# Attention into SwiGLU on one core: seven half-size products for 16 more chunks, with every side step placed by a written list

## The chip, the cores and the metric

One core of a Trainium2 chip runs the whole program. The metric is the device time of one execution, in microseconds (us); the kernel before took 926.79 us as the median of three runs (926.09 to 927.77).

## The reference, cut to what matters

```python
# q, k, v: (B=8, H=8, S=576, D=64); keys and values are averaged over windows of 8 -> 72 per head
k_p = k.reshape(B, H, 72, 8, D).mean(axis=3);  v_p = v.reshape(B, H, 72, 8, D).mean(axis=3)
scores = np.matmul(q, k_p.transpose(0, 1, 3, 2)) / np.sqrt(D)
attn = np.exp(scores - scores.max(-1, keepdims=True));  attn = attn / (attn.sum(-1, keepdims=True) + 1e-9)
x = np.matmul(attn, v_p).transpose(0, 2, 1, 3).reshape(4608, 512)      # B*S tokens, H*D channels
g = x @ w_gate                                                        # (512, 1536)
out = (g * sigmoid(g) * (x @ w_val)) @ w_out                          # (1536, 512)
```

All is float32, and the result has to be close to float32. The kernel gets there with pairs of 16-bit numbers (high part and remainder): a product of two such pairs is three matmuls, high times high, high times remainder, remainder times high.

## The kernel before, in words

**Tiles and chunks.** The 4,608 tokens are 9 tiles of 512. The 1,536 hidden channels are 12 chunks of 128. For each tile, chunk after chunk, TensorE makes the gate and the value of 128 hidden channels (both from the 512 input channels), ScalarE, VectorE and GpSimd make the hidden product from them, and TensorE multiplies that by w_out into four PSUM accumulators (`project`, L963: 4 matmuls of the float32 weights with `hh`, then 8 of 16-bit weights with `hb` and `hl`).

**Two ways to make gate and value of a chunk.** The plain way (`side`, L927 to L929) is 12 matmuls with 512 columns for the gate and 12 for the value. The other way (`product`, L1109) treats input channels, gate and value, and the two halves of the tile's tokens as a 2 by 2 block product and makes it from seven products of half the size instead of eight: 7 x 6 = 42 matmuls with 256 columns. It needs sums and differences: of the weights of a chunk (`fast_weights`, once per chunk) and of the tile's input (`fast_x`, once per tile, in two halves). Per chunk it also needs three copies on ScalarE (`keep_fast` L1424, `seed_fast` L1429, L1488) and two additions on VectorE (`second_fast` L1435, L1492), and its remainder `hl` (L1400) is made on GpSimd instead of VectorE. `READY` gives the number of chunks that go this way in each tile: 5, 7, 9, 9, 9, 9, 12 in tiles 2 to 8. A tile's plain chunks come first. Tile 8 has no plain chunk; its first products begin inside the last chunk of tile 7 (`CROSS`, `begin_fast`).

**The side work.** While TensorE works on tile i, the attention of later tiles' tokens is made, in pieces of at most 128 queries: split the queries (`split_q` L611 to L614), scores on TensorE (L631, L632), less the maximum (L641, L642), exponentials (L653), split them into a `half` buffer (`blocks_high` on ScalarE, the remainders `blocks_low` on GpSimd, L727 and L730), transpose that by a DMA (`turned` L734, `pt<-half` or `pt<-area`), multiply by the values on TensorE (`values_of_heads` L755, L756), divide (L760), split again (L882, L885) and transpose into `x` by a DMA (L890). Each batch also needs its keys and values loaded and summed (`batch_load`, `batch_sum`, `prep`).

**What sets the order.** The order is fixed when the program is built, one queue per engine (PE TensorE, ACT ScalarE, DVE VectorE, POOL GpSimd, SP the DMA queue). The first tile goes by a written list (`ORDER`). From tile 1 on the builder calls `slot` (L1170) between groups of matmuls. It keeps running counts of when each engine will be free (`now`, `spend`), and puts in what fits the room that it is told (`ROOM`, `FAST_ROOM`): sums first, then attention steps and batch steps. Two pieces at most are under way, and the `half` buffers alternate until tile 7 (`SOLO`); from there one of them serves as room for a second tile's input sums.

Of the kernel before, what the change touches and what calls it, by code (L numbers as in the profile page):

```python
# [16 lines left out]
P = 128  # L17
# [34 lines left out]
H8 m9 P8 t14 y12 La2 O12 u14 v14 w13 m10 Pa5 T8 w14 y13 O13 Y8 X8 Z8 y14 Z6 Pa2 A A  # L52
"""
AFTER = {"V": 91312.0, "A": 89862.0, "P": 94264.0}
# [3 lines left out]
EVEN_ON_VECTOR = ('N0', 'N4', 'N8')  # L58
TILE = 512
# [11 lines left out]
CAME = 6000  # L71
URGE = (0, 0)
FAST_ROOM = (3500, 1350), (2550, 2210), (1250, 1050), (950, 180), (3350, 800), (1760, 4190), (2900, 5200)
FAST_FIRST, FAST_THEN = 3, 5
ONE_BANK = (1, 8)
LANDS = 6250
SETTLE = 0
TURNS = 4500
AHEAD = 9
COST = (1.0, 1.0, 0.92)  # L80
# [20 lines left out]
def attention_then_swiglu(  # L101
# [226 lines left out]
    prepped, scaled = set(), set()  # L328
    busy = {"ps": False, "values": False, "sums": False}
# [158 lines left out]
    freed = [0, 0, 0]  # L488

    def batch_load(b, i):  # L490
        src, n, _, _ = batch(b, i)
        state["in", b, i] = mid.tile([P, 2, n], F32, name="in", tag="mid")
        nc.sync.dma_start(out=state["in", b, i], in_=src)
        state["from", b, i] = now["pe"]
        now["loads"] += 1

    def batch_sum(b, i, part=None):
        box(0)
        if i >= 4:
            box(1)  # L500
        for n in (0, 1) if part is None else (part,):
            if i >= 4:
                batch(b, i)[3](state["in", b, i], n)
            elif n == 0:
                batch(b, i)[3](state["in", b, i])
        if part != 0:
            state["in", b, i] = None
            now["loads"] -= 1
            if i < 4:
                spend("P", 2600)  # L510
            freed.append(now["P" if i < 4 else "V"] + SETTLE)

    def prep(b):

        order = 0, 4, 1, 5, 2, 6, 3, 7
        todo = [i for i in order if ("in", b, i) not in state]

        def load():
            if todo and now["loads"] < 2 and not now["hold"] and now["pe"] >= freed[-3]:
                batch_load(b, todo.pop(0))  # L520

        for i in order:
            while (
                i in todo
                or state["in", b, i] and now["pe"] < state["from", b, i] + LANDS
                or i < 4 and any(e["t"][0] == "x" for e in lines["extra"])
            ):
                load()
                yield 0, 0
            for n in (0, 1) if i >= 4 else (None,):  # L530
                if state["in", b, i]:
                    yield (batch(b, i)[2], 0, "same") if n else (batch(b, i)[2], 0)
                    batch_sum(b, i, n)
                    load()
        yield from settle("P")
        mx, ks, vs = state["sizes", b]["t"], home["ks"], home["vs"]
        yield 1300, 0
# [3 lines left out]
        yield 0, 0  # L541
        yield from settle("V")
        while busy["ps"] or (now["one"] and busy["values"]):
            yield 0, 0
        busy["sums"] = True
        sums = over_rows(mx[:, :3])
        yield 400, 0
        pow2_above(p2s[:, b, :3], inv[:, b], sums)
        yield from settle("V")
        busy["sums"] = False  # L550
# [4 lines left out]
        scaled.add(b)  # L555
        while b - 2 in under_way:
            yield 0, 0
        for g in range(2):
            yield (1100, 0, "same") if g else (1100, 0)
            split_k(b, g)  # L560
        for g in range(2):
            for part in range(4):
                yield 650, 0, "same"
                split_v(b, g, part)
        prepped.add(b)

    queries = {}
    now = {"one": False, "job": None, "pe": 0, "V": 0, "A": 0, "P": 0, "loads": 0, "hold": False}

    def spend(engine, n, *after):  # L570
        now[engine] = max(now[e] for e in (engine, "pe", *after)) + n * COST["VAP".index(engine)]

    def settle(*engines, more=SETTLE):
        end = max(now[e] for e in engines) + more
        while now["pe"] < end:
            yield 0, 0
# [198 lines left out]
    def ask(t):  # L775

        i, off, b, s0, m = t["at"]
        t["me"] = turn[0]
        turn[0] += 1
        t["qs"] = box(t["me"])["qs"] if b >= SPLIT else None  # L780
        for g in range(2 if b >= SPLIT else 0):
            for part in range(2):
                yield (0, 700, "same") if g + part else (0, 700)
                split_q(b, s0, m, t["qs"], g, part)
            spend("P", 1080, "A")
        if b >= SPLIT:
            load_next()
            yield from settle("P")

    def front(t):  # L790

        i, off, b, s0, m = t["at"]
        yield 0, 0
        while busy["values"] or busy["sums"]:
            yield 0, 0
        busy["ps"] = True
        sc = None
        for groups in ((0,), (1,)) if now["one"] else ((0, 1),):
            pss = scores(b, s0, m, t["qs"], groups=groups)
            if groups[-1]:  # L800
                if b < SPLIT:
                    load_next()
                t["asked"] = False
            for g in groups:
                yield 900, 0
                sc = less_max(b, m, pss, sc, (g,))
            yield from settle("V")
        busy["ps"] = False
        t["sc"] = sc

    last = {"turned": 0}

    def soft(t):

        i, off, b, s0, m = t["at"]
        half, sc = halves[t["me"] % 2 if now["tile"] < SOLO else 0], t["sc"]
        while now["tile"] >= SOLO and now["pe"] < last["turned"]:
            yield 0, 0
        yield 0, 900
        if b < SPLIT:  # L820
            exponentials(m, sc)
            yield from settle("A")
            yield 1300, 0
            ri = inverse_sums(m, sc)
            yield 750, 0, "same"
            normalise(nc.vector, m, sc, ri)
            yield from settle("V")
            yield 0, 1500
            soft_high(m, sc, half)
            soft_low(m, sc, half)  # L830
            spend("P", 1700, "A")
        else:
            weights(b, m, sc)
            for part in range(4):
                yield 0, (650, 450, 450, 650)[part], "same"
                blocks_high(m, sc, half, part)
            blocks_low(m, sc, half)
            spend("P", 1700, "A")
        yield 0, 0
        t["pt"] = turned(m, half, OLD // P if b < SPLIT else 2 * H)  # L840
        t["turned"] = last["turned"] = max(now["pe"], now["P"]) + TURNS
        if b >= SPLIT:
            yield 750, 0
            sm = row_sums(m, sc)
            yield 600, 0, "same"
            t["ri"] = one_over(m, sm)

    def back(t):

        i, off, b, s0, m = t["at"]  # L850
        yield 0, 0
        while now["pe"] < t["turned"]:
            yield 0, 0
        bs = sorted({sub[1] for sub in tiles[i][2]})
        while not scaled.issuperset(bs) or b not in prepped or any(busy.values()) or now["tile"] < i - 1:
            yield 0, 0
# [3 lines left out]
        if i not in rate:  # L860
            rate[i] = scales(bs, x["mt"])
        r = rate[i][b]
        busy["values"] = True
        if b < SPLIT:
            ps = values(b, m, t["pt"])
            yield 0, 700
            x_high(ps, m, x, off, r)
            yield from settle("A")
            yield 750, 0
            x_low(ps, m, x, off, r)  # L870
            yield from settle("V")
            busy["values"] = False
        else:
            ps = values_of_heads(b, m, t["pt"])
            yield 700, 0
# [728 lines left out]
```

## Time and profile before

| | |
|---|---|
| median of three runs | 926.79 us (926.09 to 927.77) |
| profiled execution, device time | 926.48 us |
| its span | 924.1 us |
| busy: TensorE matmul / weight load | 886.9 / 586.4 us |
| busy: VectorE / ScalarE / GpSimd | 638.0 / 513.8 / 462.7 us |
| granted TensorE clock, mean | 0.996 |

The span runs from the first to the last instruction; the device time is 2.4 us longer. The profile's line numbers are those of the kernel before. The order rows of the change have its own numbers: L1042 is `product`, L916 `project`, L1005, L1009 and L1020 `fast_x`, L741 the transposition of `half`, L853 that into `x`.

### The profile page before, as it was taken

The page shows a single profiled execution, that of the slowest core. Times are in us where ns is not written, and L with a number is a line of the kernel's source. Part 1 is how long each engine was busy: PE and PEld are TensorE (multiplying, and loading weights), DVE is VectorE, ACT ScalarE, POOL GpSimd, SP SyncE. Part 2 cuts the span into 40 slices and gives each one's busy share as a digit, 9 for nine tenths or more (in the row PEclk, how much of TensorE's full clock was granted, in tenths as well). Part 3 has the DMA queues.
Part 4 walks back from the last instruction along what each step waited for, and adds up shares of the span by engine and source line. Part 5 has one row for each costly group of instructions (what it writes and reads, how often), then busy time and mean ns, then how long its engine had stood idle before and what let it go on. Part 6 is the DMA issues. An engine that isn't in the chain of part 4 may idle for free.

```text
span 924.1 us, 16885 instructions
## 1 busy us (share of the span) xinstructions
PE 886.9 (96%) x6414; PEld 586.4 (63%) x6505; DVE 638.0 (69%) x1155; ACT 513.8 (56%) x1081; POOL 462.7 (50%) x520
## 2 busy tenths in 40 slices
PE   4789999999999999999999999999999999999997
PEld 4676445454555575577667765776577757777775
DVE  6899985877767679676867777677755585634233
ACT  2677833375456555746475655665657555444343
POOL 5457966498666944776376332543214416114111
PEclk9899999999999999999999999999999999999999
DMA  9967742257443822863286236732322322101001
GB/s 348 261 221 229 251 117 71 73 170 158 80 140 52 221 57 56 205 154 78 47 192 162 64 71 171 164 91 40 96 54 63 76 69 41 29 1 46 1 1 46
DMA packets 155537, 103.19 MB, mean 112 GB/s; under 512 B 113216, under 2 KB 141888, under 8 KB 153920
## 3 DMA queue, kind: packets, MB, share of 16 engines
q1 hardware_dynamic: 153728, 83.24, 37.4%
q10 hardware_dynamic: 1728, 18.88, 5.5%
q8 instruction: 51, 0.84, 0.4%
q14 instruction: 30, 0.25, 0.1%
HBM read 67.63 MB, written 9.44 MB: 83 GB/s over the span
## 4 chain that ended last, share of the span: by engine, by line
PE 76%; DVE 15%; issue 3%; ACT 2%; DMA 2%; POOL 2%; SPq 0%; ACTq 0%; DVEq 0%; POOLq 0%
PE gv L1109 29%; PE acc L963 24%; PE gv L927 6%; PE gv L929 6%; PE gv L928 6%; DVE mixed L244 2%; DVE wgv_l L278 1%; DVE hf L945 1%; DMA qt<-q_rows 1%; PE ps L631 1%; DVE ws L233 1%; DVE hf L951 1%; PE ps L755 1%; PE ps L632 1%; DVE fx L1057 1%
## 5 line engine op out<-in xcount | busy, mean ns | idle before, releaser
L1400 POOL TENSOR_TENSOR hl<-hf,hh 128x512 bf16<-128x512 f32 x71 | 92.9, 1309 | 198.3 <-ACT hh L1391 198.3
L941 ACT ACTIVATE hf<-gv,un 128x512 f32<-128x512 f32 (+1 forms) x111 | 75.0, 675 | 171.7 <-PE gv L1109 111.8
L963 PE MATMUL acc<-hl,wo_h 128*128 128x512 bf16 (+1 forms) x435 | 161.4, 373 | 2.2 <-issue 0.3
L945 DVE SCALAR_TENSOR_TENSOR hf<-hf,gv 128x512 f32<-128x512 f32 (+1 forms) x111 | 74.4, 670 | 119.3 <-ACT hf L941 119.2
L927 PE MATMUL gv<-x,wgv_h 128*128 128x512 f16 (+1 forms) x408 | 149.6, 367 | 4.5 <-DVE hf L945 3.8
L929 PE MATMUL gv<-x,wgv_l 128*128 128x512 f16 (+1 forms) x408 | 149.5, 366 | 0.5 <-DVE wgv_l L278 0.5
L928 PE MATMUL gv<-x,wgv_h 128*128 128x512 f16 (+1 forms) x408 | 149.5, 366 | 0.5 <-DVE x L770 0.5
L963 PE MATMUL acc<-hh,wo_h 128*128 128x512 f32 (+1 forms) x444 | 130.1, 415 | 0.0
L614 POOL TENSOR_TENSOR box<-qt,box 64x512 f16<-64x512 f32 (+1 forms) x60 | 66.5, 1109 | 105.6 <-ACT box L613 91.8
L963 PE MATMUL acc<-hb,wo_l 128*128 128x512 bf16 x307 | 117.2, 382 | 0.4
L1109 PEld LDWEIGHTS <-mixed 128*128 128x128 f16 x1044 | 101.1, 98 | 25.5 <-issue 0.9
L1109 PEld LDWEIGHTS <-wgv_h 128*128 128x128 f16 x960 | 92.9, 98 | 34.2 <-issue 2.4
L1391 ACT CAST hh<-hf 128x512 fp32r<-128x512 f32 x72 | 44.4, 617 | 117.8 <-DVE hf L951 117.7
L1109 PE MATMUL gv<-area,mixed 128*128 128x256 f16 x696 | 94.9, 273 | 0.0
L1109 PE MATMUL gv<-x,wgv_h 128*128 128x256 f16 x528 | 93.0, 273 | 0.0
L951 DVE SCALAR_TENSOR_TENSOR hf<-gv,un,hf 128x512 f32<-128x512 f32 (+1 forms) x87 | 63.3, 728 | 39.6 <-PE gv L1109 34.0
L963 PEld LDWEIGHTS acc<-hh,wo_h 128*128 128x128 f32 x444 | 76.3, 189 | 14.0 <-ACT hh L1391 0.3
L963 PEld LDWEIGHTS <-wo_l 128*128 128x128 bf16 x444 | 43.2, 97 | 52.1 <-issue 26.3
L1109 PE MATMUL gv<-x,wgv_l 128*128 128x256 f16 x264 | 71.9, 273 | 0.0
L929 PEld LDWEIGHTS <-wgv_l 128*128 128x128 f16 x408 | 39.9, 98 | 44.7 <-DVE wgv_l L278 1.0
L928 PEld LDWEIGHTS <-wgv_h 128*128 128x128 f16 x408 | 39.9, 98 | 42.8 <-issue 5.2
L927 PEld LDWEIGHTS <-wgv_h 128*128 128x128 f16 x408 | 39.9, 98 | 38.1
(203 smaller groups left out, 1883.7 us busy)
## 6 DMA issues: line engine op xcount, KB each, us to landing
ws<-w_all ACTq DMA_DIRECT2D x12, 1536.0 KB, 7.2
qt<-q_twice SPq DMA_DIRECT2D x48, 256.0 KB, 3.1
out_t<-ob SPq DMA_DIRECT2D x36, 256.0 KB, 2.5
in<-k_rows SPq DMA_DIRECT2D x12, 576.0 KB, 5.1
in<-q_rows SPq DMA_DIRECT2D x12, 576.0 KB, 5.1
in<-v_main SPq DMA_DIRECT2D x12, 512.0 KB, 5.0
in<-v_rest SPq DMA_DIRECT2D x12, 512.0 KB, 5.0
qt<-q_rows SPq DMA_DIRECT2D x8, 256.0 KB, 6.2
```

The source lines that it names most:

```text
L244: nc.vector.scalar_tensor_tensor(out=wf.bitcast(U32), in0=wf.bitcast(U32), scalar=3, in1=chunks[c]["low"], op0=ALU.logical_shift_left, op1 ...
L614: nc.gpsimd.tensor_sub(o[rows], qt[rows], o[rows])
L927: nc.tensor.matmul(o, wh, x["h"][:, j, a:e], start=(j == 0), stop=False)
L928: nc.tensor.matmul(o, wh, x["l"][:, j, a:e], start=False, stop=False)
L929: nc.tensor.matmul(o, wl, x["h"][:, j, a:e], start=False, stop=(j == NJ - 1))
L941: nc.scalar.activation(hf, gate, AF.Tanh, scale=un[:, c, 0:1])
L945: nc.vector.scalar_tensor_tensor(out=hf, in0=hf, scalar=1.0, in1=gate, op0=ALU.add, op1=ALU.mult)
L951: nc.vector.scalar_tensor_tensor(out=out, in0=val, scalar=un[:, c, 2:3], in1=hf, op0=ALU.mult, op1=ALU.mult)
L963: nc.tensor.matmul(acc[j][:, a:e], w[:, c, j * P : (j + 1) * P], h[:, :n], start=begin and at < NJ, stop=end and w is wo_up,)
L1109: nc.tensor.matmul(o, a, b, start=begin and j + n == 0, stop=j == HJ - 1 and n == 2, skip_group_check=True,)
L1391: nc.scalar.copy(hh[:, :n], hf)
L1400: eng.tensor_sub(hl[:, :n], hf, hh[:, :n].bitcast(F32))
```

## The change

`READY` becomes 7, 10, 11, 12, 12, 12, 12 for tiles 2 to 8: 16 more chunks by seven half-size products, 76 instead of 60. Tiles 5, 6 and 7 have no plain chunk any more, so their first products, like those of tile 8, begin inside the last chunk of the tile before. One `half` buffer is given up from tile 4 on instead of tile 8 (`SOLO` 3). The running counts go. `slot` now takes its steps from a written list, one group of steps per place, with finer steps: p for a piece of attention, b and l for a batch and its loads, w and x for the sums of weights and of a tile's input, q for the loads of queries.

```diff
-ROOM = (3410, 3290)
-READY = (0,0,5,7,9,9,9,9,12)
-MADE = (0,5,7,9,9,9,9,11)
-LATE = {8:(11,)}
-CROSS = (8,)
-SOLO = 7
+READY = (0, 0, 7, 10, 11, 12, 12, 12, 12)
+CROSS = (5,6,7,8)
+SOLO = 3
+PLAN = """
+p0:2 w0 / w0:3 / w0 b2 p0 / / w0 / / w0 / p0 b2:3 / / / q w0 p0 b2 / / p0 b2:2 p1 w0 / p1 b2 w0
...
-    def slot(vector, scalar):
-        room = {"V": now["pe"] + vector, "A": now["pe"] + scalar}
...
+    steps_of = iter(PLAN.split("/"))
+    def slot():
+        for word in next(steps_of).split():
+            name, _, times = word.partition(":")
+            for _ in range(int(times or 1)):
+                if name not in lines:
+                    lines[name] = line(name)
+                next(lines[name], None)
...
-        while now["tile"] >= SOLO and now["pe"] < last["turned"]:
-            yield 0, 0
...
-        while now["pe"] < t["turned"]:
-            yield 0, 0
...
-            while now["pe"] < came[i][n]:
-                yield 0, 0
```

The step functions issue the same instructions as before (`ask`, `front`, `soft` and `back` are joined into `attend`); only where they stand differs, and a `yield` now ends a step without asking for room. At the end of `ORDER` the two steps `A`, which began the next batch, are gone.

On TensorE, at the start of tile 7, a plain chunk's gate stands before, right behind tile 6's last `project`:

```order
L963 MATMUL acc_7889<-hl,wo_h 128x512
L927 LDWEIGHTS wgv_h
L927 MATMUL gv_8915<-x,wgv_h 128x512
L928 LDWEIGHTS wgv_h
L928 MATMUL gv_8915<-x,wgv_h 128x512
L929 LDWEIGHTS wgv_l
L929 MATMUL gv_8915<-x,wgv_l 128x512
```

and now tile 7's first product of half the size, one chunk earlier in the queue:

```order
L1042 MATMUL gv_9226<-x,wgv_h 128x256
L1042 LDWEIGHTS wgv_h
L1042 MATMUL gv_9226<-x,wgv_h 128x256
L1042 LDWEIGHTS wgv_l
L1042 MATMUL gv_9226<-x,wgv_l 128x256
```

The matmuls have 256 columns where they had 512, and each still has its own weight load.

On VectorE, around the start of tile 7 (`un` marks it). Before, tile 7's input sums (`fx<-x`, `fx<-fx`) follow it:

```order
L951 SCALAR_TENSOR_TENSOR hf<-gv_8782,un,hf 128x512
L1446 TENSOR_TENSOR un<-p2w,mt 128x36
L1057 TENSOR_TENSOR fx<-x 128x2x256 x2
L1064 TENSOR_TENSOR fx<-fx 128x2x128 x4
L908 TENSOR_SCALAR mt<-p2s 128x1
```

Now the second half of these sums stands in the next to last chunk of tile 6, cut in pieces between the chunk's own four operations (L900, L1339, L905, L1293):

```order
L1293 TENSOR_TENSOR gv_9075<-gv_9030,rs 128x256
L666 TENSOR_REDUCE sm<-sc 128x8
L1005 TENSOR_TENSOR fx<-x 128x2x256 x2
L1009 TENSOR_TENSOR fx<-fx 128x2x128 x2
L900 SCALAR_TENSOR_TENSOR hf<-hf,gv_9075 128x512
L1339 TENSOR_TENSOR gv_9030<-gv_9030,rs 128x256
L1009 TENSOR_TENSOR fx<-fx 128x2x128 x2
L905 SCALAR_TENSOR_TENSOR hf<-gv_9030,un,hf 128x512
L1293 TENSOR_TENSOR gv_9173<-gv_9131,rs 128x256
L1020 TENSOR_TENSOR x<-fx,x 128x2x128
L1020 TENSOR_TENSOR area<-fx,area 128x6x128
```

On the DMA queue, the end of tile 6 and the start of tile 7 (`out_t<-ob` writes a finished tile). Before, the transpositions of `half` alternate between two buffers, and the last one into tile 7's `x` stands well behind it:

```order
L584 DMA qt<-q_twice 128x4x128 x2
L734 DMA_TRANSPOSE pt<-area 128x16x64
L584 DMA qt<-q_twice 128x4x128 x2
L734 DMA_TRANSPOSE pt<-half 128x16x128
L890 DMA_TRANSPOSE x<-box 128x8x64
L584 DMA qt<-q_twice 128x4x128 x2
L734 DMA_TRANSPOSE pt<-area 128x16x128
L1121 DMA out_t<-ob 128x512 x4
```

Now all go through one buffer, and the last one into `x` (of 64 queries) has the next piece's transposition right ahead of it:

```order
L741 DMA_TRANSPOSE pt<-half 128x16x64
L853 DMA_TRANSPOSE x<-box 128x8x64
L591 DMA qt<-q_twice 128x4x128 x2
L741 DMA_TRANSPOSE pt<-half 128x16x128
L853 DMA_TRANSPOSE x<-box 128x8x64
L741 DMA_TRANSPOSE pt<-half 128x16x128
L591 DMA qt<-q_twice 128x4x128 x2
L1053 DMA out_t<-ob 128x512 x4
```

The input of tile 7 is now finished and summed before tile 6 ends.

## Rows read from the trace of the kernel before

**Rows 1.** The page: the span and the busy time of each engine.

```profile
span 924.1 us, 16885 instructions
PE 886.9 (96%) x6414; PEld 586.4 (63%) x6505; DVE 638.0 (69%) x1155; ACT 513.8 (56%) x1081; POOL 462.7 (50%) x520
```

**Rows 2.** Busy time of each engine by stretches that are about the tiles (1 to 8 from the second row on); columns: stretch, its length, busy us (instructions) of PE, PEld, DVE, ACT and POOL, granted TensorE clock, DMA share, GB/s.

```profile
0.00:138.00 138.00, 113.64 (x829) 77.27 (x833) 121.35 (x213) 84.03 (x164) 88.23 (x102) 0.98 0.76 239
138.00:258.00 120.00, 118.19 (x704) 61.01 (x711) 87.97 (x147) 58.56 (x116) 83.30 (x93) 1.00 0.45 109
258.00:358.00 100.00, 98.77 (x684) 59.89 (x695) 70.96 (x127) 57.93 (x124) 62.10 (x74) 1.00 0.47 112
358.00:453.00 95.00, 94.08 (x679) 61.48 (x690) 70.47 (x129) 58.50 (x127) 61.12 (x70) 1.00 0.53 124
453.00:548.00 95.00, 94.04 (x742) 65.41 (x753) 68.64 (x129) 58.65 (x129) 52.02 (x58) 1.00 0.52 119
548.00:641.00 93.00, 92.40 (x715) 64.71 (x724) 68.96 (x134) 54.04 (x117) 37.18 (x41) 1.00 0.48 115
641.00:736.50 95.50, 94.60 (x745) 65.75 (x754) 59.38 (x117) 57.48 (x129) 29.84 (x34) 1.00 0.32 70
736.50:831.60 95.10, 94.19 (x705) 66.06 (x715) 59.12 (x111) 48.77 (x103) 29.04 (x32) 1.00 0.15 34
831.60:924.00 92.40, 87.01 (x626) 64.85 (x635) 31.18 (x55) 35.84 (x76) 19.90 (x19) 1.00 0.07 24
```

**Rows 3.** The timeline of TensorE: the first and the last of the twelve matmuls of one plain gate (start, duration, line).

```profile
560.00 0.38 PE L927 MATMUL gv<-x,wgv_h 128*128 128x512 f16 x1
...
562.38 0.38 PE L929 MATMUL gv<-x,wgv_l 128*128 128x512 f16 x1
```

**Rows 4.** The chain of waits in tile 8, in order of time: start, length, what, and how many in a row.

```profile
839.09 2.62 PE gv L1109 x24
...
846.34 2.62 PE gv L1109 x24
```

**Rows 5.** Groups of instructions by form: the weight loads of the half-size products (busy us, mean ns of one, idle before).

```profile
L1109 PEld LDWEIGHTS <-mixed 128*128 128x128 f16 x1044 | 101.1, 98 | 25.5 <-issue 0.9
```

**Rows 6.** The same view: what a chunk costs beside TensorE. Three copies, two additions, the remainder on either engine, and VectorE's two other operations.

```profile
L1424 ACT COPY rs<-gv 128x256 f32<-128x256 f32 x60 | 22.8, 380 | 0.0
L1429 ACT COPY gv<-gv 128x256 f32<-128x256 f32 x60 | 22.3, 372 | 5.0 <-DVE hf L945 3.9
L1488 ACT COPY gv<-gv 128x256 f32<-128x256 f32 x60 | 21.7, 361 | 0.7 <-PE gv L1109 0.4
L1435 DVE TENSOR_TENSOR gv<-gv,rs 128x256 f32<-128x256 f32 x60 | 25.8, 430 | 47.6 <-PE gv L1109 42.6 <-ACT hb L1394 2.8 <-PE ps L213 1.5
L1492 DVE TENSOR_TENSOR gv<-gv,rs 128x256 f32<-128x256 f32 x60 | 25.6, 426 | 2.0 <-ACT gv L1488 2.0
L1400 DVE TENSOR_TENSOR hl<-gv,hh 128x512 bf16<-128x512 f32 x24 | 16.5, 688 | 15.1 <-ACT hb L1394 15.1
L1400 POOL TENSOR_TENSOR hl<-hf,hh 128x512 bf16<-128x512 f32 x71 | 92.9, 1309 | 198.3 <-ACT hh L1391 198.3
L945 DVE SCALAR_TENSOR_TENSOR hf<-hf,gv 128x512 f32<-128x512 f32 x105 | 71.9, 685 | 119.3 <-ACT hf L941 119.2
L951 DVE SCALAR_TENSOR_TENSOR hf<-gv,un,hf 128x512 f32<-128x512 f32 x81 | 60.5, 746 | 39.6 <-PE gv L1109 34.0 <-PE gv L929 3.9 <-POOL wo_l L287 1.0
```

**Rows 7.** The same view: the sums of a tile's input on VectorE with the copy on ScalarE.

```profile
L1057 DVE TENSOR_TENSOR fx<-x 128x512 f32<-128x512 f16 x28 | 20.6, 777 | 0.0
L1064 DVE TENSOR_TENSOR fx<-fx 128x256 f32<-128x256 f32 x32 | 16.8, 525 | 0.8
L1077 ACT CAST x<-fx 128x256 f16<-128x256 f32 x2 | 0.8, 405 | 0.0
L1083 DVE TENSOR_TENSOR x<-fx,x 128x256 f16<-128x256 f32 x2 | 1.8, 891 | 0.6 <-ACT x L1077 0.6
```

**Rows 8.** The page: the DMA transpositions, how many and the median us from issue to landing.

```profile
x<-box SPq DMA_TRANSPOSE x30, 3.6
pt<-half SPq DMA_TRANSPOSE x21, 4.3
```

**Rows 9.** The timeline of GpSimd, the DMA queue and the weight loads at one place of tile 4: the remainders of a piece, its transposition, and the first weight load that reads it, with TensorE's idle time before it in brackets.

```profile
473.25 1.15 POOL L727 TENSOR_TENSOR half<-sc,half 64x512 f16<-64x512 f32 x1
474.36 0.44 POOL L730 TENSOR_TENSOR half<-sc,half 64x32 f16<-64x32 f32 x2
474.82 1.24 SPq L734 DMA_TRANSPOSE pt<-half  x1
478.36 0.11 PEld L755 LDWEIGHTS <-pt 128*64 128x64 f16 x1 [0.55 <-DMA pt<-half]
```

**Rows 10.** Groups by form: the first operation of a chunk's weight sums on VectorE and of four such on GpSimd.

```profile
L1019 DVE TENSOR_TENSOR fw<-wgv_h,wgv_l 128x1024 f32<-128x1024 f16 x12 | 15.1, 1255 | 0.0
L1021 POOL TENSOR_TENSOR fw<-fw 128x256 f32<-128x256 f32 x12 | 8.7, 728 | 21.2 <-DVE fw L1019 21.2
```

More of the change, by code (lines that the diff above doesn't have):

```diff
@@ L77 @@
[L77 to L80, printed above, removed]
 def _plan(nt, s):
@@ L507, in batch_sum, with batch_loads @@
             state["in", b, i] = None
[L508 to L511, printed above, removed]
[L513 to L529 removed]
+    IN_TURN = 0, 4, 1, 5, 2, 6, 3, 7
+    def batch_loads(b):
+        for i in IN_TURN:
+            if ("in", b, i) not in state:
+                batch_load(b, i)
+                yield
+    def prep(b):
+        for i in IN_TURN:
             for n in (0, 1) if i >= 4 else (None,):
                 if state["in", b, i]:
[L532 removed]
                     batch_sum(b, i, n)
[L534 to L535 removed]
+                    yield
         mx, ks, vs = state["sizes", b]["t"], home["ks"], home["vs"]
[L537 removed]
         nc.vector.tensor_reduce(out=mx[:, 0:1], in_=mx[:, 3:7], axis=AX.X, op=ALU.max)
@@ L540, in prep @@
         largest(mx[:, 2:3], vs)
-        yield 0, 0
-        yield from settle("V")
-        while busy["ps"] or (now["one"] and busy["values"]):
-            yield 0, 0
-        busy["sums"] = True
+        yield
         sums = over_rows(mx[:, :3])
-        yield 400, 0
+        yield
         pow2_above(p2s[:, b, :3], inv[:, b], sums)
-        yield from settle("V")
-        busy["sums"] = False
+        yield
         nc.vector.tensor_scalar(
@@ L554, in prep @@
         )
-        scaled.add(b)
-        while b - 2 in under_way:
-            yield 0, 0
         for g in range(2):
-            yield (1100, 0, "same") if g else (1100, 0)
             split_k(b, g)
+            yield
         for g in range(2):
             for part in range(4):
-                yield 650, 0, "same"
                 split_v(b, g, part)
-        prepped.add(b)
+                yield
     queries = {}
[L568 to L576, printed above, removed]
+    now = {"one": False, "job": None, "tile": 0}
     def load_q(b, s0, n):
@@ L773, in x_low, with attend @@
         )
[L775 to L780, printed above, removed]
+    def attend(p):
+        i, off, b, s0, m = ahead[p]
+        me = turn[0] + p
+        qs = box(me)["qs"] if b >= SPLIT else None
         for g in range(2 if b >= SPLIT else 0):
             for part in range(2):
[L783 to L796, printed above, removed]
+                split_q(b, s0, m, qs, g, part)
+                yield
         sc = None
         for groups in ((0,), (1,)) if now["one"] else ((0, 1),):
[L799 to L803, printed above, removed]
+            pss = scores(b, s0, m, qs, groups=groups)
@@ L804, in front @@
+            yield
             for g in groups:
-                yield 900, 0
                 sc = less_max(b, m, pss, sc, (g,))
[L807 to L816, printed above, removed]
-        while now["tile"] >= SOLO and now["pe"] < last["turned"]:
-            yield 0, 0
-        yield 0, 900
+                yield
@@ L832, in soft @@
         else:
             weights(b, m, sc)
+            yield
             for part in range(4):
-                yield 0, (650, 450, 450, 650)[part], "same"
                 blocks_high(m, sc, half, part)
+                yield
             blocks_low(m, sc, half)
[L838 to L841, printed above, removed]
+            yield
+        pt = turned(m, half, OLD // P if b < SPLIT else 2 * H)
@@ L842, in soft @@
+        yield
         if b >= SPLIT:
-            yield 750, 0
             sm = row_sums(m, sc)
[L845 to L851, printed above, removed]
-        while now["pe"] < t["turned"]:
[L853 to L856, printed above, removed]
+            yield
+            ri = one_over(m, sm)
+            yield
@@ L1202, in next_batch, with asked_queries, line @@
-    def next_batch(room):
-        if not lines["prep"] and now["batch"] < B:
-            b = now["batch"]
-            if b <= now["tile"] + 2 and sum(piece[2] < b for piece in ahead) <= AHEAD:
-                join("prep", prep(b))
-                now["batch"] += 1
-        forward("prep", room)
+    lines = {}
+    def asked_queries():
+        for p in range(1, len(ahead)):
+            load_q(*ahead[p][2:])
+            yield
+    def line(name):
+        n = int(name[1:] or 0)
+        if name[0] == "q":
+            return asked_queries()
+        return {"p": attend, "b": prep, "l": batch_loads, "w": fast_weights, "x": fast_x}[name[0]](n)
@@ L1416, in begin_fast @@
             product(t["x"], 1, c, k, False)
-            if c == ready(k) - 1 and SOLO < k + 1 < len(tiles) and ready(k + 1) < NCH and not left[k + 1]:
-                summed.add(k + 1)
-                join("extra", fast_x(k + 1), ("x", k + 1))
             return t
```

313 lines of the change are left out of this document (116 added, 197 removed).

## The prediction

> **What bounds the kernel now.** First the engines' share of the span: TensorE is busy 886.9 us of 924.1, the next engine, VectorE, 638.0 [rows 1]. A share is an average, so next the stretches by tile [rows 2]. The idle time is at the ends: 24.4 us in tile 0 (138.00 - 113.64) and 5.4 in tile 8, most of it the way out of the last tile. In tiles 2 to 7 TensorE is idle 1.2, 0.9, 1.0, 0.6, 0.9 and 0.9 us, 5.5 in all. So in these tiles only two things change the time: the length of TensorE's own queue, and waits that do not exist yet. The granted clock is 1.00 in every stretch from tile 1 on, its upper level, and the change gives TensorE no pause longer than it has there, unless a rival below comes true; I enter nothing for the clock.
>
> The profiled execution took 926.48 us (span 924.1 and 2.4 outside it). My sum is made against that; the median of the runs is 0.3 higher.
>
> **A. TensorE's queue, 16 chunks: -9.7.** A plain chunk is 24 matmuls with 512 columns for gate and value. In the timeline the first and the twelfth start 2.38 us apart, eleven steps of 0.2164 us [rows 3]. 24 x 0.2164 = 5.19 us. The other way is 42 matmuls with 256 columns. In the chain of tile 8, 24 of them in a row last 2.62 us, 0.1092 each [rows 4]; 42 x 0.1092 = 4.59. The difference is 0.61 us per chunk, 9.7 for 16. Both prices are from start to start with the weight loads among them, so the 18 further loads per chunk are paid in the 0.1092: a load of 98 ns [rows 5] lies beside a matmul of 109. It is a tight fit, and the gain is one eighth of the arithmetic less that fit: 42 half matmuls would be 4.54 at half of 0.2164.
>
> **B. What a chunk costs beside TensorE: 0.** By [rows 6], each of the 16 adds 0.380 + 0.372 + 0.361 = 1.11 us on ScalarE, 0.430 + 0.426 - 0.688 = +0.17 on VectorE (the remainder leaves it) and 1.31 on GpSimd. Tile 5 gets three chunks: ScalarE 58.65 + 3.3, VectorE 68.64 + 0.5, GpSimd 52.02 + 3.9, in 95 us [rows 2]. What hides this is TensorE's own chunk: from one to the next in tile 8 it is 846.34 - 839.09 = 7.25 us [rows 4], while VectorE's four operations of a chunk are 0.685 + 0.430 + 0.746 + 0.426 = 2.29. If the cover were gone on VectorE, a chunk would wait for what else stands in its queue; that is part of C and of rival 1.
>
> **C. Input sums at the tile boundaries: +1.0 (0 to +6.0).** A tile that begins with half-size products waits for the whole of its input and its sums: last transposition into `x`, then on VectorE two sums of 0.777 and four of 0.525, a copy of 0.405 on ScalarE and a last sum of 0.891 [rows 7], the transposition itself 3.6 [rows 8]. That is 3.6 + 1.55 + 2.10 + 0.41 + 0.89 = 8.55 us, and 10.84 where the chunk's own 2.29 stands between. Before tiles 6 and 8 the changed order leaves 20 us and more of TensorE's queue behind that transposition. Before tiles 5 and 7 there are only 42 half and 15 whole matmuls: 42 x 0.1092 + 15 x 0.2164 = 7.83 us. So they may be short by 0.7 to 3.0 us each, 6.0 for both. The lower end is 0: what feeds the transposition is placed one chunk earlier than it is needed, and only if its turn comes late does the shortfall show. I take 0.5 each, nearer to 0, as the pieces stand between the chunk's operations and not behind them.
>
> **D. The transposed exponentials: +2.0 (0 to +16).** With one `half` buffer a piece's remainders cannot be written before the previous piece's transposition is done, and the written list sets how far the values stand behind them. I count TensorE's queue between a piece's last remainder on GpSimd and its first product with the values. In nine places it holds 6.5, 6.3, 7.4, 7.2, 6.8, 6.1, 7.2, 7.4 and 5.2 us; before, the shortest were 7.2 and 7.9. What has to fit in: the remainders, 1.15 + 0.44 = 1.6, and the transposition, at [rows 9] 478.36 - 474.82 = 3.5 from issue to the first load that reads it: 5.2 us with a moment for the issue, and then nothing is late anywhere (0). But at [rows 9] TensorE was 0.55 us idle although it had the 7.9: GpSimd began late. If GpSimd is as late at all nine, 7.9 + 0.55 = 8.45 are needed and the nine lack 2.0, 2.2, 1.1, 1.3, 1.7, 2.4, 1.3, 1.1 and 3.3, 16 in all (the median landing of these transpositions, 4.3 [rows 8], lies between). I take 2.0, close to the lower end: GpSimd has under 80% to do in every tile, and at most places it is free when a piece comes.
>
> **Steps that move to other tiles: 0.** The number of chunks whose weights are summed stays 12, but three of those sums move from tiles 7 and 8 to tiles 2 to 5, and the input sums of tiles 5 to 7 move one chunk or more ahead. A weight sum is 1.255 us on VectorE and at least 4 x 0.728 on GpSimd [rows 10]; its other groups of operations I take as no longer, some 5.5 us in all. VectorE in the fullest tile goes from 71 to about 75 of 95 to 100 us and GpSimd in tile 2 from 62 to under 80. Cost on the path 0 as long as each stands behind the chunk's own four operations; the written list spreads them over the chunks.
>
> **E. Old waits that go: -1.0 (0 to -5.5).** Of the 5.5 us that tiles 2 to 7 were idle [rows 2], those on the way into tiles 5 to 7 go with the earlier sums. The rest returns elsewhere.
>
> **Sum:** -9.7 + 0 + 1.0 + 2.0 - 1.0 = -7.7, so 926.48 - 7.7 = 918.8 for an execution like the profiled one, and 919.0 as the median of runs. Ends: 926.48 - 9.7 - 5.5 = 911.3; with 6.0 and 16 us of waits 938.8.
>
> A measurement of this kernel can tell about 0.2%, 1.9 us, from no change.
>
> **Rivals**
> 1. *The boundaries cost their full price.* VectorE comes to the sums with the chunk's operations between and begins late; tiles 5 and 7 each wait 3.0. For it: 7.83 us against a chain of 10.84. Against: the sums' first half is done long before, and their input stands one chunk early. 926.48 - 9.7 + 6.0 + 1.0 (D and E together) = 923.8.
> 2. *Slower: the transposed exponentials are late nearly everywhere.* One mechanism: the single `half` buffer. GpSimd cannot begin a piece's remainders until the piece before has left the buffer, the values stand where the list put them, and TensorE, in order, stands still with all half-size products behind. At full price 926.48 - 9.7 + 16 = 932.8. It decides from the point where the nine waits together exceed 9.7 + 1.9 = 11.6, 1.3 each. For it: the 0.55 at [rows 9] and nine places tighter than nearly all of before. Against: the same chain took 5.2 where GpSimd was free. The running counts used to wait until the transposition was due; the list does not, so a late one is not moved but waited for.
> 3. *Slower: weight loads beside nothing.* If a load did not lie beside the matmul ahead of it, a product with 256 columns would cost 0.109 + 0.098 and a whole one 0.216 + 0.098, and the change would add 16 x (42 x 0.207 - 24 x 0.314) = 18.5: 945.0. The rows speak against it: 24 products with 24 loads of 98 ns lasted 2.62 us, not 5.0 [rows 4, 5]. The Trainium skill, page "TensorE: Matmul & The Clock Gate", section "The mechanism" (Part 3), lists that a weight load overlaps with matmuls in flight only when its row group differs, though it also excepts loads into a background buffer; by the list's rule, with loads for the whole array as here, this rival would be the forecast. The trace does not agree with that rule.
>
> That the change does not do what it says I count at nothing: the order holds 16 x 36 = 576 more rows on TensorE.
>
> **How the numbers follow.** The forecast, 915 to 922: 0.72, all faster. Rival 1: 0.14; around 923.8, of which 0.09 below 924.9 (faster) and 0.05 within 0.2%. Rival 2: 0.12, of which 0.11 slower and 0.01 within. Rival 3: 0.02, slower. Faster 0.81, same 0.06, slower 0.13. Time 919.0. The range reaches down to 914.5, where E gives back most of its 5.5 and C and D cost a little (-9.7 - 4 + 1.7), and up to 926.0, which takes in rival 1 and leaves out most of rival 2.
>
> **What would show it.** Right: TensorE busy about 877 us; a stretch of 24 half-size products still 2.62 us; tiles 5, 6 and 7, with three more such chunks each, about 1.8 us shorter; waits of the values on `pt` under 3 us in all, of tile 5's and 7's first products on `x` under 2. Wrong: step A if a half-size product takes over 0.115 where weight loads are dense; step C if TensorE's first products of tiles 5 and 7 wait some 3 us on VectorE or ScalarE; step D if loads of `pt` wait over 10 us in all behind GpSimd's remainders; step B if chunks wait on VectorE within tiles 2 to 5; and the clock, if the waits let it fall below 1.00.

## The result, and the profile after

The change makes the kernel **slower**: 936.83 us as the median of four runs (935.93 to 938.40), against 926.47 for the kernel before in the same comparison (926.09 to 927.77). The ratio is 1.0111, with a 95% interval of 1.0093 to 1.0129. The forecast was 919.0, in a range of 914.5 to 926.0. The profiled execution of the change took 937.21 us, with a span of 935.4.

The page of the changed kernel: span and busy time, which answer to [rows 1].

```profile
span 935.4 us, 17628 instructions
PE 888.4 (95%) x6793; PEld 615.7 (66%) x6793; DVE 651.4 (70%) x1171; ACT 526.4 (56%) x1129; POOL 486.0 (52%) x536
```

TensorE is busy 888.4 us, not 877. But a matmul of 512 columns is drawn 0.38 us long while the next one can start after 0.2164 [rows 3], so a pause of up to 0.16 us still counts as busy here. The waits say more. First the changed kernel's, then some of the kernel before's (eight rows in all), both from 138 us on, that is without tile 0. The columns are who waited for whom, us in total, times, longest.

```profile
PE gv L1042 <- DVE gv L1339: 12.8, 17, 1.9
PE gv L1042 <- DVE x L1020: 2.4, 3, 1.2
PE ps L763 <- DVE box L436: 1.1, 1, 1.1
PE ps L638 <- DVE sc L767: 1.0, 2, 0.5
PE ps L762 <- DVE sc L767: 0.8, 1, 0.8
PE gv L1042 <- ACT gv L1288: 0.3, 1, 0.3
```

```profile
PE gv L1109 <- DVE gv L1492: 1.0, 3, 0.7
PE ps L631 <- POOL box L614: 0.8, 1, 0.8
PE ps L631 <- DVE x L770: 0.4, 1, 0.4
...
PE ps L755 <- DMA pt<-area: 0.2, 1, 0.2
```

L1339 of the change is L1492 of before: the second of a chunk's two additions on VectorE. Product 4, the last of the chunk's seven to be issued, waits for it in both kernels. It stands right behind the gating (L900, before L945), which multiplies ScalarE's tanh plus one by the gate. This one wait went from 1.0 us in 3 places to 12.8 in 17. All of the change's rows make 18.4 us in 25 waits; with the 0.16 that each hides, 22.4. The kernel before has 3.5 in 11, so 5.3. The difference is 17.1. It has to explain 21.0: the span is 11.3 longer, and the 9.7 of term A are to be made up. Another 1.6 is already lost when tile 1 has its first product with w_out (172.4 against 170.8 us); in the twelve traces of this case, which share the first tile's list, that product starts anywhere from 169.8 to 172.5, so these 1.6 cannot be laid to the change. For the 2.3 that are left I found no row.

What such a wait looks like: VectorE of the changed kernel in tile 4, from a chunk's first addition (L1293; the expectations call it the third) to the same chunk's gating (L900) and second addition (L1339), and TensorE at the same place.

```profile
473.43 0.43 DVE L1293 TENSOR_TENSOR gv<-gv,rs 128x256 f32<-128x256 f32 x1 [1.06 <-PE gv L1042]
473.78 0.44 DVE L648 TENSOR_REDUCE mx<-ps 64x4 f32<-64x288 f32 x1
474.25 0.45 DVE L649 TENSOR_TENSOR sc<-ps,mx 64x288 f32<-64x288 f32 x1
474.62 2.31 DVE L336 TENSOR_REDUCE box<-in 128x72 f32<-128x576 f32 x2
476.86 0.73 DVE L848 SCALAR_TENSOR_TENSOR box<-sc,r,box 128x512 f16<-128x512 f32 x1
477.52 0.55 DVE L434 TENSOR_SCALAR box<-box,inv 64x256 f16<-64x256 f32 x1
478.10 1.37 DVE L436 SCALAR_TENSOR_TENSOR box<-box,inv 8x256 f16<-8x256 f32 x1
479.50 0.69 DVE L900 SCALAR_TENSOR_TENSOR hf<-hf,gv 128x512 f32<-128x512 f32 x1
480.11 0.42 DVE L1339 TENSOR_TENSOR gv<-gv,rs 128x256 f32<-128x256 f32 x1
```

```profile
478.55 0.38 PE L916 MATMUL acc<-hb,wo_l 128*128 128x512 bf16 x1
480.59 0.38 PE L1042 MATMUL gv<-area,wgv_h 128*128 128x256 f16 x2 [1.66 <-DVE gv L1339]
```

The written list puts a step of the scores, two batch sums, an attention remainder and two steps of a batch's split there, 5.9 us. TensorE starts product 4 0.06 us behind the addition's end, 2.04 us after its matmul before, where 0.2164 would do. The same stretch in tile 8 of the changed kernel, where the list has nothing, shows how much fits:

```profile
857.50 0.43 DVE L1293 TENSOR_TENSOR gv<-gv,rs 128x256 f32<-128x256 f32 x1 [1.06 <-PE gv L1042]
860.84 0.69 DVE L900 SCALAR_TENSOR_TENSOR hf<-hf,gv 128x512 f32<-128x512 f32 x1 [2.91 <-ACT hf L897]
861.44 0.42 DVE L1339 TENSOR_TENSOR gv<-gv,rs 128x256 f32<-128x256 f32 x1
```

VectorE idles 2.91 us until the gating can start, and the addition ends at 861.86, 0.22 before product 4 starts at 862.08. So **about 3.1 us** of other work fit ahead of a chunk's gating, not 7.25 less 2.29. Counted over the trace, by the summed durations of what stands between L1293 and the gating: more than 3.3 us stood there in 1 of 60 chunks before and in 23 of 76 now. At 16 of those 23 TensorE waited, 10.5 us in all, at the other 53 chunks 7 times, 2.7 us (the rows above leave out waits under 0.15 us).

Three stretches of the changed kernel, in the columns of [rows 2]:

```profile
258.00:358.00 100.00, 96.30 (x722) 61.99 (x721) 78.68 (x139) 61.60 (x133) 74.09 (x89) 1.00 0.48 114
453.00:548.00 95.00, 89.90 (x753) 65.33 (x751) 73.31 (x138) 58.42 (x132) 47.58 (x51) 1.00 0.48 119
548.00:641.00 93.00, 88.75 (x762) 67.30 (x760) 73.94 (x135) 54.22 (x121) 44.24 (x47) 1.00 0.42 107
```

TensorE now idles 3.7, 5.1 and 4.3 us in stretches where it idled 1.2, 1.0 and 0.6. VectorE is at 80% at most. The granted clock is 1.00 in all three, so it plays no part there.

### The profile page after: what moved, and what is told of

The parts are those of the page before. It is cut to its first block, busy times and chain, and to the rows that moved or that the text cites. A ratio compares the mean times of both kernels' runs of the same rounds, so it can differ in the third digit from the quotient of the medians.

```text
span 935.4 us, 17628 instructions
## 1 busy us (share of the span) xinstructions
PE 888.4 (95%) x6793; PEld 615.7 (66%) x6793; DVE 651.4 (70%) x1171; ACT 526.4 (56%) x1129; POOL 486.0 (52%) x536
## 5 line engine op out<-in xcount | busy, mean ns | idle before, releaser
L1270 POOL TENSOR_TENSOR hl<-hf,hh 128x512 bf16<-128x512 f32 x87 | 113.1, 1300 | 279.7 <-ACT hh L1263 279.7
L1042 PEld LDWEIGHTS <-wgv_h 128*128 128x128 f16 x1216 | 116.8, 98 | 56.2 <-issue 20.2
L900 DVE SCALAR_TENSOR_TENSOR hf<-hf,gv 128x512 f32<-128x512 f32 (+1 forms) x111 | 74.2, 669 | 109.2 <-ACT hf L897 106.5
L916 PE MATMUL acc<-hb,wo_l 128*128 128x512 bf16 x384 | 146.5, 382 | 0.0
L1042 PE MATMUL gv<-x,wgv_h 128*128 128x256 f16 x800 | 139.7, 273 | 2.4 <-DVE x L1020 2.4
L1042 PE MATMUL gv<-x,wgv_l 128*128 128x256 f16 x400 | 109.0, 273 | 0.0
L905 DVE SCALAR_TENSOR_TENSOR hf<-gv,un,hf 128x512 f32<-128x512 f32 (+1 forms) x103 | 75.1, 730 | 43.7 <-PE gv L1042 38.7
L884 PE MATMUL gv<-x,wgv_h 128*128 128x512 f16 (+1 forms) x280 | 101.0, 361 | 4.5 <-DVE hf L900 3.8
L885 PE MATMUL gv<-x,wgv_h 128*128 128x512 f16 (+1 forms) x280 | 101.0, 361 | 0.5 <-DVE x L777 0.5
L886 PE MATMUL gv<-x,wgv_l 128*128 128x512 f16 (+1 forms) x280 | 101.0, 361 | 0.5 <-DVE wgv_l L322 0.5
L916 PEld LDWEIGHTS acc<-hh,wo_h 128*128 128x128 f32 x444 | 75.9, 189 | 13.4 <-ACT hh L1263 0.3
L1293 DVE TENSOR_TENSOR gv<-gv,rs 128x256 f32<-128x256 f32 x76 | 32.8, 431 | 57.0 <-PE gv L1042 53.9
L1042 PE MATMUL gv<-area,wgv_h 128*128 128x256 f16 x304 | 53.9, 272 | 13.2 <-DVE gv L1339 12.8
L1042 PEld LDWEIGHTS <-wgv_l 128*128 128x128 f16 x608 | 59.4, 98 | 9.8 <-issue 2.9
```

The costliest lines, as they stand in the source:

```text
L884: nc.tensor.matmul(o, wh, x["h"][:, j, a:e], start=(j == 0), stop=False)
L885: nc.tensor.matmul(o, wh, x["l"][:, j, a:e], start=False, stop=False)
L886: nc.tensor.matmul(o, wl, x["h"][:, j, a:e], start=False, stop=(j == NJ - 1))
L900: nc.vector.scalar_tensor_tensor(out=hf, in0=hf, scalar=1.0, in1=gate, op0=ALU.add, op1=ALU.mult)
L905: nc.vector.scalar_tensor_tensor(out=out, in0=val, scalar=un[:, c, 2:3], in1=hf, op0=ALU.mult, op1=ALU.mult)
L916: nc.tensor.matmul(acc[j][:, a:e], w[:, c, j * P : (j + 1) * P], h[:, :n], start=begin and at < NJ, stop=end and w is wo_up,)
```

## The experiments

The theory, **Q**: the list bunches VectorE's side steps ahead of the addition that product 4 waits for. The rivals: **H**, the single half buffer; **F**, VectorE and GpSimd have too much to do with 16 more chunks, wherever it stands. Each result is given beside the kernel before in the same comparison (926.07, 926.07, 925.81 and 926.06 us in the four).

**1. The same steps at other places** (`e1_moved`). Of the list's 1,144 steps 306 move by one to six places; their sequence, the chunks and the buffer stay. Seven places around the wait shown above:

```diff
-p15 p14 l6 q p15 b6 l6 p17 / p15 b6 p13 b6 / p15 p14 b5 l6 / p16 b6 b5 / / / l6
+b6 l6 p17 / p15 / / / b6 p13 b6 p15 / p14 b5 l6 / p16 b6
```

(The first five words stand a place earlier now, the last ones, `b5 l6`, a place later.)

> The changed kernel with the same steps in the same sequence, and the same 16 further chunks and single half buffer; 306 of the list's 1,144 steps stand one to six places earlier or later, so that VectorE has no more than about 3.3 us of them between a chunk's third addition (L1293) and the one that product 4 waits for (L1339). Theory Q (steps bunched on VectorE ahead of L1339 hold TensorE): the 12.8 us of waits on L1339 go, and most of the 2.9 on the input sums and 2.3 on the values with them, so 912 to 922 us. Rival H (the single half buffer): its transpositions stay, not under 930. Rival F (VectorE and GpSimd have too much to do with 16 more chunks, wherever it stands): not under 930.

Measured: 926.98 us, ratio 1.0007 (0.9995 to 1.0018). That is 9.9 better than the change, with the same 16 chunks and the same buffer: against H and F, which had it not under 930. But it is 5 to 15 short of what Q expected. In 8 of the 76 chunks more than 3.3 us still stand ahead of the gating, and waits on the addition (here L1340) are left in five places:

```profile
PE gv L1043 <- DVE gv L1340: 7.3, 5, 4.0
```

The longest, 4.0 us, is of this placing's own making. A query split stood on ScalarE earlier than its load landed, and the chunk's tanh (L898) behind it:

```profile
306.67 0.72 ACT L619 ACTIVATE qt<-qt,inv 128x512 f32<-128x512 f32 x1 [5.39 <-DMA qt<-q_twice]
...
307.95 0.68 ACT L898 ACTIVATE hf<-gv,un 128x512 f32<-128x512 f32 x1
```

**2. The addition first** (`e2_add_first`).

```diff
-                    if not final:
-                        gated(hf, gate)
                     nc.vector.tensor_add(t["x"], t["x"], t["rs"])
-                    if final:
-                        gated(hf, gate)
+                    gated(hf, gate)
```

> The changed kernel with VectorE's addition L1339 ahead of the chunk's gating L900 instead of behind it. Theory Q1 (only the operation right ahead of the addition makes it late): each of the 22 waits on it shrinks by up to 0.67 us, 8.9 in all, so about 928 us. Theory Q2 (VectorE's whole queue is late in these chunks, so what the addition gains the gating and what follows lose): within 2 us of the changed kernel's 936.8. Rivals H and F: no change either.

Measured: 929.20 us, ratio 1.0039 (1.0026 to 1.0052), 7.6 better than the change. The waits on the addition (L1337 here) fell from 12.8 us in 17 places to 7.6 in 9, those on the input sums from 2.4 to 1.2. Q1 is near (8.9 expected), Q2 is refuted: what the gating loses by standing second costs TensorE hardly anything. The only new row of that kind is one wait of 0.2 us, on the multiplication behind it (L905).

**3. One half buffer alone** (`e3_one_half`).

```diff
-SOLO = 7
+SOLO = 3
```

> The kernel before with one change: the half buffer is given up from tile 3 on instead of tile 7 (SOLO 3); chunks, running counts and all else as before. Theory Q: the running counts wait for the buffer, so at most 3 us slower than before, 926.5 to 929.5. Rival H: a single buffer costs TensorE most of what was lost, 935 or more.

Measured: 932.58 us, ratio 1.0060 (1.0039 to 1.0081). Both expectations missed: 6.5 us is more than Q allowed and less than H claimed. Under the running counts, which wait for the buffer, the loss is spread over many small waits: on the addition L1435 2.0 us, on L760 ahead of the values and the scores 1.5 and 0.7, on L1492 only 0.5, on a transposition hardly any:

```profile
PE gv L1109 <- DVE gv L1435: 2.0, 2, 1.5
PE ps L755 <- DVE sc L760: 1.5, 2, 0.8
...
PE ps L755 <- DMA pt<-area: 0.2, 1, 0.2
```

So the single buffer has a price where the order is made as before. In the changed kernel the rows of these kinds, on the values and the scores, are 2.9 of the 18.4 us, and none is on L1293. How much of the change's own loss passes through the buffer was not measured apart; run 8 shows that with another list the price is not paid.

**4. The kernel before, with more room** (`e4_room`). This makes the bunching without the rest of the change.

```diff
-FAST_ROOM = (3500, 1350), (2550, 2210), (1250, 1050), (950, 180), (3350, 800), (1760, 4190), (2900, 5200)
+FAST_ROOM = (5500, 1350), (4550, 2210), (3250, 1050), (2950, 180), (3350, 800), (1760, 4190), (2900, 5200)
```

> The kernel before with one change: the room in which the running counts may put steps on VectorE is 2 us larger at the four places between a half-size chunk's third addition and the one that product 4 waits for (FAST_ROOM entries 0 to 3). Chunks and both half buffers as before. Theory Q: steps bunch ahead of that addition and TensorE waits for it as in the changed kernel, 10 to 20 us slower than before, 936 to 946, the waits on L1492 over 8 us where they were 1.0. Rivals H and F: nothing that they blame is touched, within 2 us of before.

Measured: 939.31 us, ratio 1.0128 (1.0110 to 1.0147). As Q said: the waits on L1492 went from 1.0 to 11.7 us, and 12 of the 60 chunks now have more than 3.3 us ahead of the gating, where 1 had. The loss of the change is made again with 60 chunks and two buffers; neither H nor F has a reason for that.

```profile
PE gv L1109 <- DVE gv L1492: 11.7, 11, 1.8
```

**5 and 6. Both cures** (`e5_add_first_moved`, `e6_add_first_moved_more`): run 2's edit and two further placings. In the first, of the row in run 1 only the step `b5` (L436) moves behind product 4, with a load that stood there (`p16 b6 b5 / / / l6 / p17` becomes `p16 b6 / / / / b5 l6 p17`).

> The changed kernel with both cures: the addition L1339 ahead of the gating L900, and 194 of the list's 1,144 steps one to ten places earlier or later, in the same sequence. Theory Q (VectorE late at that addition): the two cures gained 7.6 and 9.9 us alone and act on the same 12.8 us of waits and on some 8 us of others, so together 916 to 923 us, 3 to 10 faster than the kernel before; the waits on the addition under 3 us in all. Rival F (VectorE and GpSimd too full): no better than the better cure alone, 927.

> As the one with both cures, but with another placing, 375 of 1,144 steps moved. Theory Q: 916 to 923 us as well, within 4 us of the other placing, since what counts is how much stands on VectorE ahead of the addition and not which steps. Rival F: 927 or more.

Measured: 921.85 us, ratio 0.9958 (0.9943 to 0.9972), and 930.21, ratio 1.0040 (1.0028 to 1.0052). The first is within Q's bounds and faster than the kernel before. The second is a miss: more than 3.3 us stand ahead of the gating in 13 of its chunks and in 15 of the first's, and yet it is 8 us behind. Its waits are other ones: 2.7 us of the scores on VectorE in tile 6, 2.4 on a transposition, 5.0 on the addition in three places, the longest again behind a query split that waits 4.48 us for its load.

```profile
PE gv L1043 <- DVE gv L1338: 5.0, 3, 2.7
PE ps L639 <- DVE sc L650: 2.7, 1, 2.7
PE ps L763 <- DMA pt<-half: 2.4, 1, 2.4
```

So "which steps" matters as well: a moved step must not come ahead of its load. That is 2.7 of the 8 us; the other waits were not followed to their cause.

**7. The same chunks by running counts** (`e7_counts`).

```diff
-READY = (0,0,5,7,9,9,9,9,12)
-MADE = (0,5,7,9,9,9,9,11)
-LATE = {8:(11,)}
+READY = (0,0,7,10,11,12,12,12,12)
+MADE = (0,7,10,11,12,12,12,12)
+LATE = {}
-CROSS = (8,)
-SOLO = 7
+CROSS = (5,6,7,8)
+SOLO = 3
```

> The kernel before with the change's numbers of chunks (7, 10, 11, 12, 12, 12, 12), its crossings of tiles 5 to 8 and its single half buffer from tile 3 on, but with the running counts instead of the written list. Theory Q: the counts keep the room ahead of the addition, so the waits on it (L1492) stay under 4 us; but a boundary then waits for its input sums, which the counts begin only when the input is there: 2 to 8 us at each of tiles 3 to 7. So 935 to 960, by other waits than the change has. Rival F: the waits on the addition are there with the counts too, 10 us or more.

Measured: 974.33 us, ratio 1.0518 (1.0500 to 1.0535), outside the 935 to 960. This kernel does not compute the right output: without `LATE` the last chunk's weight sums are written into `first` at 500.4 us (L1033), while the products of tile 4 still read that tile's input sums from it, up to 567.9 us. So it shows what the counts do with these numbers of chunks, not what a right kernel would take. The kinds of waits are the expected ones, only larger: on the addition 2.0 us, on the input sums (copies L1077, differences L1083) 31.0 in the rows shown.

```profile
PE gv L1109 <- ACT x L1077: 14.2, 3, 10.5
PE gv L1109 <- ACT first L1077: 9.6, 2, 7.3
...
PE gv L1109 <- POOL first L1083: 5.0, 2, 2.8
...
PE gv L1109 <- POOL x L1083: 2.2, 1, 2.2
PE gv L1109 <- DVE gv L1492: 2.0, 3, 1.0
```

One more wait, of 8.3 us, stands ahead of a plain gate (L927), and the profile names nothing that ended it. The granted clock is lower too, 0.975 on average against 0.995 in the change, and 0.94 to 0.97 from 258 to 680 us, where the long waits are. The counts keep the room ahead of the addition and pay at the boundaries; the list has the boundaries (2.4 us) and pays ahead of the addition.

**8 and 9. Both cures, with tile 2 repaired** (`e8_tile2_mixed`, `e9_tile2_old`). In run 5, what was left lay in tile 2, at two places where the change's own list was better. There it is put back.

> The run with both cures and 194 moved steps, but at the start of tile 2 and from its last half-size chunk to the start of tile 3 the steps stand again where the change had them (164 moved). There the moved list cost TensorE more than the change's: 2.3 us at the first addition (a query load landed late) and 1.8 at the values before tile 3, against 0 and 1.0. Theory Q: those waits fall back, the rest stays, 917 to 920.5 us. If instead each placing only shifts its waits to the next place: 921 to 924.

> As the run above, but all steps of tile 2 up to the start of tile 3 stand where the change had them (151 moved, all in tiles 3 to 7). Tile 2 then loses what it lost with the addition first alone, 5.9 us instead of the 9.0 with both cures. Theory Q: 918 to 921 us. If waits only shift: 921 to 924.

Measured: **917.75 us**, ratio 0.9914 (0.9900 to 0.9928), and 919.22, ratio 0.9934 (0.9919 to 0.9948). Both are as expected; waits do not just shift. Of run 8, the page, TensorE's waits from 138 us on, and VectorE at the place shown above:

```profile
span 915.4 us, 17672 instructions
PE 881.9 (96%) x6793; PEld 612.7 (67%) x6793; DVE 650.2 (71%) x1171; ACT 527.9 (58%) x1129; POOL 485.7 (53%) x536
```

```profile
PE ps L764 <- DVE box L437: 1.1, 1, 1.1
PE ps L763 <- DVE sc L768: 0.8, 1, 0.8
PE ps L639 <- DVE sc L650: 0.8, 1, 0.8
PE gv L1043 <- DVE gv L1338: 0.7, 1, 0.7
...
```

```profile
473.57 0.43 DVE L1338 TENSOR_TENSOR gv<-gv,rs 128x256 f32<-128x256 f32 x1 [0.42 <-ACT gv L1337]
473.91 0.68 DVE L901 SCALAR_TENSOR_TENSOR hf<-hf,gv 128x512 f32<-128x512 f32 x1
474.90 0.75 DVE L906 SCALAR_TENSOR_TENSOR hf<-gv,un,hf 128x512 f32<-128x512 f32 x1 [0.32 <-PE gv L1043]
475.69 0.50 DVE L437 SCALAR_TENSOR_TENSOR box<-box,inv 8x256 f16<-8x256 f32 x1
```

VectorE is as busy as in the change (650.2 against 651.4) and GpSimd too (485.7 against 486.0); there are 76 chunks and one half buffer. The step L437 (the change's L436) stands behind the multiplication, and VectorE is idle 0.42 us ahead of the addition, until ScalarE's copy (L1337) is done. Product 4 then starts 0.41 us after the matmul before it, so TensorE loses 0.2 us here where it lost 1.8. With the addition first, more fits ahead of it, about 3.6 us: from 857.93 to 861.6, so that it ends by 862.0. More than 3.7 us stand there in 11 chunks of run 8, still, and in 17 of the change; so the limit is not sharp. Scores and values of the attention on TensorE, mostly 8 or 16 matmuls of 0.032 us in such a stretch, lengthen it, and how much each chunk can bear was not settled. What is settled is that the same work, with 76 chunks and one half buffer, costs TensorE little at other places: 4.3 us of waits in 7 places, against 18.4 in 25 in the change and 3.5 in 11 before. This refutes F, and H as a loss that the single buffer must bring. The 8.1 us gained over the kernel before are most of term A's 9.7. Run 2's swap was not tried on the kernel before by itself; it could gain little there, as the waits on L1492 are 1.0 us in 3 places.

**10. Less on GpSimd** (`e10_less_gpsimd`), to see how much of VectorE's lateness GpSimd makes. From tile 1 on the kernel leaves out two of the three additions that sum a part of a batch's keys or values.

```diff
-        eng.tensor_add(a, a, b4)
-        eng.tensor_add(a[:, :, : 2 * inner], a[:, :, : 2 * inner], a[:, :, 2 * inner :])
+        if now["tile"] < 1:
+            eng.tensor_add(a, a, b4)
+            eng.tensor_add(a[:, :, : 2 * inner], a[:, :, : 2 * inner], a[:, :, 2 * inner :])
```

> The changed kernel, with two of the three GpSimd additions that sum a part of a batch's keys or values left out from tile 1 on (1.27 and 0.73 us each, 24 parts, some 44 us of GpSimd's 486); so keys and values of the later batches are wrong, and the list and all else are the change's. Theory Q with GpSimd's share: VectorE operations that work between buffers last longer while GpSimd runs (L436 0.47 to 1.90 us), so VectorE's busy time falls by 4 to 10 us and the waits on L1339 by 1 to 4: 932 to 936 us. If the bunching by the list alone makes VectorE late: within 1 us of 936.8. If GpSimd itself were what holds TensorE: under 930.

Measured: 934.60 us (931.34 to 937.25), ratio 1.0099 (1.0078 to 1.0120). GpSimd fell from 486.0 to 443.2 us, VectorE from 651.4 to 646.6, and the waits on the addition from 12.8 to 9.3 in the profiled execution, which was the fastest of the four. The direction is the expected one, but in time the intervals of this run and of the change overlap: GpSimd's share in the loss looks small, and this run cannot size it.

## Why the prediction was wrong, point by point

**Step A, TensorE's queue, -9.7: right.** In the changed kernel's tile 8 a run of 24 half-size products lasts 2.62 us and a chunk 7.25 (843.53 to 850.78), as in [rows 4]:

```profile
843.53 2.62 PE gv L1042 x24
...
850.78 2.62 PE gv L1042 x24
```

Once most of the waits were taken out (run 8), the kernel gained 8.1 us. Only the sign "TensorE busy about 877 us" did not come true, not even in run 8 (881.9): as said above, busy time holds short pauses too. Rival 3, weight loads beside nothing, is out: by it no version with 16 more such chunks could gain.

**Step B, side work at 0: this is the step that failed.** It named the cover as "TensorE's own chunk", 7.25 us against 2.29 of VectorE's own. The cover is narrower. Of these 7.25 us only about 3.1 lie ahead of the gating and the addition that product 4 waits for; work behind product 4 cannot borrow from them. The step compared sums per tile and per chunk with a chunk's length, and the price of the list is set by what stands in one stretch of it. The trace of before showed the stretch: in its tile 8 VectorE idles 2.91 us ahead of the gating, and with the room of the counts 59 of 60 chunks had at most 3.3 us there:

```profile
856.40 0.69 DVE L945 SCALAR_TENSOR_TENSOR hf<-hf,gv 128x512 f32<-128x512 f32 x1 [2.91 <-ACT hf L941]
857.00 0.43 DVE L1492 TENSOR_TENSOR gv<-gv,rs 128x256 f32<-128x256 f32 x1
```

Put at 0, it costs 12.8 us by the rows, 15.5 with 17 x 0.16. "The written list spreads them over the chunks" was asserted and not counted: 23 of 76 chunks are over. VectorE's busy time grew by 13.4 us and not by 16 x 0.17 = 2.7, although the operations added are those that the step counted (32 more additions, 16 fewer remainders). The rest is operations that last longer, as the last section shows.

**Step C, input sums, +1.0: a size too small, within its range, and the places wrong.** The waits on L1020 are 2.4 us in three places, 2.9 with what each hides, and stand ahead of tiles 6, 7 and 8 (647, 743 and 836 us). The step had looked for them ahead of tiles 5 and 7, by counting TensorE's work behind the last transposition; ahead of tiles 6 and 8 it had counted 20 us and more. What made VectorE's sums late there was not followed.

**Step D, transposed exponentials, +2.0: the size came out, but by luck.** The values waited 1.1 and 0.8 us in two places (L763, L762), and what they waited for was VectorE again; no wait of theirs on a transposition has a row among the waits of TensorE's matmuls.

**Steps that move, 0:** part of step B's failure, as input and weight sums (L1005, L1009, L1020, L970) are among the bunched steps: some 23 of the 95 us that stand in those 23 stretches. **Step E, -1.0:** not seen; the idle time of tiles 2, 4 and 5 grew.

**The rivals.** The time came out on the slower side, as rival 2 had it (932.8, chance 0.12), but by another mechanism: not transpositions out of the single half buffer. Its sentence that the list "is not moved but waited for" where the counts would wait holds, only for VectorE's queue. No rival was a late VectorE within the chunks, although the words on what would show step B wrong named it.

## What to carry to other kernels

Work beside a saturated engine is not hidden by the length of a round but by the stretch between two points at which that engine waits for its helper; find each such stretch where the helper is idle, measure it (here about 3.1 of 7.25 us, and not the same in every chunk), and add up what a new order puts into it, place by place. Averages per tile do not show it: VectorE at 70% cost TensorE 15 us at the addition here, and at 71% only 0.7 there in run 8. An operation that the saturated engine waits for belongs ahead of one that it does not wait for soon (run 2: 7.6 us for one swapped line). And a step moved ahead of its load holds its queue and what waits for it (4.0 us in run 1, 2.7 in run 6).

## What the hardware showed that was not expected

Many VectorE operations that read and write SBUF buffers only, and not PSUM, last longer when they meet GpSimd. In the changed kernel from 130 us on L436 took 0.47 to 0.48 us where no GpSimd operation overlapped it (3 times) and 0.47 to 1.90 where one did (9 times, mean 1.14), L848 0.74 and 1.03 on average. The gating, which reads PSUM, took 0.67 to 0.69 in both cases. The reductions do not last longer although they stay within SBUF (L666 0.73 to 0.75). At 478.10, above, L436 ends 0.28 us after the GpSimd operation that it met:

```profile
477.88 1.31 POOL L341 TENSOR_TENSOR in<-in 128x512 f32<-128x512 f32 x1
```

Summed over tiles 1 to 8 of the changed kernel, VectorE's operations last 55 us longer than the shortest of their form (differences over 0.1 us), in the kernel before 42. That is most of the 13.4 us by which VectorE's busy time grew; GpSimd's grew by 23.3 (462.7 to 486.0). The Trainium skill, page "SBUF — State Buffer", section "SBUF: two separate sides", has a rule for this: certain VectorE operations and GpSimd's share a port pair, and whichever starts first keeps it for its whole instruction. The trace agrees with it here, with the 0.28 us above; run 10 moved VectorE's busy time by 4.8 us for 42.8 us less on GpSimd. The steps that bunched are mostly of this kind, so a stretch that just fits on paper may not fit beside GpSimd.
